# A fused attention and two-FFN kernel: three float64 weight blocks decoded in attention and not four, a first FFN that begins with two groups of two blocks, sums of values on GpSimd

## The chip, the core and the metric

One core of a Trainium2 chip runs the whole program. The metric is device time in microseconds (us) per execution; the times below are medians over runs. The core has five engines that work on their own queues and wait for each other through semaphores: TensorE (PE in the profile; its weight loads are PEld), VectorE (DVE), ScalarE (ACT), GpSimd (POOL) and SyncE (SP, which issues the DMAs).

## What is computed

```
mask   = q_bucket[:, :, :, None] == k_bucket[:, :, None, :]   # 6 sign bits of q@proj, k@proj
scores = where(mask, q @ k.T / 8, -1e9)                       # 2 batches, 8 heads, 768 x 768, d = 64
attn   = softmax(scores) @ v                                  # -> x: 1536 tokens x 512
h = x @ w_in; x = (h * tanh(softplus(h))) @ w_out             # first FFN, d_ff 2048, float64 weights
P = exp(x @ w_gate - max); 8 rounds of row and column normalising
out = sum over 8 experts e of  P[:, e] * (relu(x @ w1[e]) @ w2[e])   # d_ff 1024 each
```

[...] All large products run in fp32r, a reduced format of TensorE; an operand is split into a high part and the rest (`hi`, `lo`), and three products are added.

## The kernel before, in words

**Attention** (`attention()`, 32 units: 16 heads with two halves of 384 queries) is not written in the order in which it runs. Each piece of work is registered as a task with an engine (or two to choose from), a planned cost, a due time and the tasks that it follows; a greedy list scheduler at the end of the function takes the earliest one and emits it. So a task that changes its engine or cost shifts others too. Each unit has score tiles with row maxima (`s_mm`, `s_max`), transposed scores and their exponential (`st_mm`, `st_exp`), a split of the exponential (`split_hi`, `split_lo`), the product with the values (`av_count`, `av_mm`) and a normalisation (`norm`). A row whose bucket matches no key needs the plain sum over all values of its head: `vsum_red` adds up the six value chunks of two heads, `vsum_mm` adds over partitions, `vsum_fin` splits, `vsum_move` stores.

**Float64 decoding.** The first FFN has 16 blocks of 128 hidden columns; a block is 128 x 1024 words, loaded in two halves. `decode` turns a half into float32 in nine parts: sign (L135), absolute value (L137 on VectorE or L139 on ScalarE), low word (L141, ScalarE), clamp (L143), exponent (L147), sign back (L151), scale of the low word (L155), a product (L157, GpSimd) and a sum into `dec` (L159, VectorE). Then `convert_hi` (L171, ScalarE) writes the high part of a block into its place in a ring of 8 (`w0` to `w7`, of which `wx0` is number 2), and `convert_lo` (L176, GpSimd) the rest. In attention, `decode` tasks for the first `NATT` = 4 blocks are among those that the scheduler places, half n due at 10 + 11n; blocks 0 to 2 are also converted there, block 3 right after attention.

**First FFN** (the loop over `n` at the end of the listing). It is written in steps. A step is one weight block with one of three token blocks (`tb`, 512 tokens): `up(n)`, 12 matmuls into PSUM (L787 to L789: high weight with `xh`, high weight with `xl`, low weight with `xh`), `act(n)` (Mish and a cast on ScalarE L799, L800, the rest on VectorE L801), and `down` of step n - 3, 12 matmuls (L823) that add to four PSUM banks `y0` to `y3`. Blocks form `GROUPS` of four: a group goes over the three token blocks, and after its last block of a token block the four banks are added into `acc` by `evacuate` (the first group copies on ScalarE, L831; others add on VectorE, L833). In such a step `down` and `evacuate` stand ahead of `act`.

The remaining blocks are decoded in the steps: a list `early` gives each half a step d; parts 0 to 4 are written after `up(d)`, parts 5 to 7 at the end of step d, the last one at the end of step d + 1. A block is converted at the end of step d + 2 of its second half, behind whatever parts stand in that step. In the table below "decoded" gives the steps d of the two halves.

After it come a gate with its normalisation, expert 0 of both halves in the same loop (steps 48 to 71), and experts 1 to 7 in a Strassen form (L1122, L1185).

Of the kernel before, what the change touches and what calls it, by code (L numbers as in the profile page):

```python
# [7 lines left out]
F32 = mybir.dt.float32  # L8
# [5 lines left out]
ALU = mybir.AluOpType  # L14
AX = mybir.AxisListType

P = 128
B, H, S, D = 2, 8, 768, 64
# [10 lines left out]
NTB = NTOK // TB  # L29
BIG = float(2 ** 33)  # L30
N64 = 16
# [10 lines left out]
DUE0 = 10  # L42
PACE = 11
NX = 1
NATT = 4
FG = 4
LOW64 = float(2.0 ** -15)
HIGH64 = float(122880.0)
# [1 line left out]
RING_A = 2  # L50
# [7 lines left out]
def lsh_attention_moe_kernel(  # L58
# [13 lines left out]
    nc = tc.nc  # L72
# [23 lines left out]
    NW = N64 + NF  # L96
# [72 lines left out]
    def convert_hi():  # L169
        i = converted[0]  # L170
        nc.scalar.copy(ring[i % RING][:, 0, :], source(i))  # L171

    def convert_lo():
        i = converted[0]
        dst = ring[i % RING]
        nc.gpsimd.tensor_sub(dst[:, 1, :], source(i), f32(dst[:, 0, :]))  # L176
        converted[0] += 1
        if i >= N64:
            staged.pop(i)
            load_next()  # L180


    def attention():
        with ExitStack() as a:
# [4 lines left out]
            vs_p = a.enter_context(tc.tile_pool(name="vsp", bufs=1))  # L189
# [33 lines left out]
            vs_t = [None] * 4  # L223
# [126 lines left out]


            def vsum_red(h):
                vs_t[0] = vs_p.tile([P, 2, D], F32, tag="vs", name="vs")
                nc.vector.tensor_reduce(  # L354
                    out=vs_t[0], in_=vt[h // 2 % 2][:, :, 0:3:2, :].rearrange("p c a d -> p a d c"), axis=AX.X, op=ALU.add
                )

            def vsum_mm(h):
                vs_t[1] = ps_m.tile([P, 512], F32, tag="m", name="pvs")
# [165 lines left out]
            def task(engine, cost, due, f, *args, after=(), lag=None, ring=None, frees=None):  # L525
                tasks[f.__name__, *args] = (engine, cost, due, f, args, list(after), lag, ring, frees)
# [28 lines left out]
            for h in range(NH):  # L555
# [31 lines left out]
                task("Q", 0.6, vdue - 10, load_v, h, after=freed + [nm(clear, "vt", h // 2 % 2)] + [nm(prep_move, 0, j) for j in range(2, 6)] * (h < 2) + [nm(prep_move, 1, j) for j in range(6)] * (1 < h < 4), lag=1.3)  # L587
                if h % 2:
                    first = h >= 3
                    task("D", 0.9, vdue, vsum_red, h, after=[nm(load_v, h - 1), nm(load_v, h)] + [nm(vsum_mm, h - 2)] * first)  # L590
                    task("E", 0.11, vdue + 1, vsum_mm, h, after=[nm(vsum_red, h), nm(clear_start)], ring="m", frees=nm(vsum_fin, h))
                    task("D", 0.4, vdue + 2, vsum_fin, h, after=[nm(vsum_mm, h)] + [nm(vsum_move, h - 2, j) for j in range(2) if first])
                    for j in range(2):
                        task("Q", 0.6, vdue + 2.5, vsum_move, h, j, lag=0.01,
                             after=[nm(vsum_fin, h), nm(clear_start), nm(count_rows, 0), nm(count_rows, 1)]
                             + ([nm(av_count, 2 * prev + 1)] if prev >= 0 else []))
# [172 lines left out]
    hps, hid, yps = {}, {}, {}  # L769
    NST = NTB * NW  # L770

    GROUPS = [list(range(i, i + FG)) for i in range(0, NW, FG)]
    steps = [(g, tb, i) for g, c in enumerate(GROUPS) for tb in range(NTB) for i in c]
    NG = N64 // FG

    def step(n):
        g, tb, i = steps[n]
# [139 lines left out]

    LAG = 3
    blk = NTB * NF
    start_e = NG * NTB * FG  # L920
    for tb in range(NTB):
        n0 = start_e - (NTB - 1 - tb) * FG + LAG + 2
        at(n0, put(f"l{tb}", lambda tb=tb: logits(tb)))
# [118 lines left out]
    nxt = 0  # L1042
    nd = 0.0
    free_dec = {}
    convert_hi()
    convert_lo()
    for i in range(RING_A + NX + 1, NW):
        need = free[i - RING] + 1 if i >= RING else 0
        if NATT <= i < N64:
            nd = max(nd, free_dec.get(i - NDEC, 0))  # L1050
            for j in range(2):
                d = int(nd)
                for part, lag in enumerate((0, 0, 0, 0, 0, 0.5, 0.5, 0.5, 1.4)):
                    early.setdefault(d + lag, []).append((i, j, part, "D"))
                nd += 1.5
            need = max(need, d + 2)
        nxt = max(nxt, need)
        t = nxt
        at(t, convert_hi)
        at(t, convert_lo)  # L1060
        free_dec[i] = nxt + 1
        nxt += 1
# [247 lines left out]
```

## Time and profile before

| what | value |
|---|---|
| time, median of 3 runs | 1593.63 us (1593.13 to 1595.21) |
| the profiled execution | 1594.76 us; its span 1593.0 us |
| busy shares of the span | PE 98%, PEld 84%, DVE 54%, ACT 40%, POOL 54% |
| chain that ended last | PE 88%, DVE 8%, DMA 2%, issue 1%, ACT 1% |
| attention, then first FFN | 0 to 301.2 us, then steps of 24 matmuls |

The profile is one execution. "Busy" counts time with an instruction under way; for PE the ends of matmuls are modelled, so that overlapping matmuls fill its row. The chain is followed back from the last instruction, at each step to what released it. The difference between the execution's time and its span, 1.76 us, lies before the first and after the last instruction.

### The profile page before, as it was taken

The numbers are of one execution on the slowest core, as the hardware profiler recorded it, in microseconds if no ns is written. First come the engines' busy times: TensorE is split into PE (matmuls) and PEld (weight loads), VectorE is DVE, ScalarE is ACT, GpSimd is POOL, SyncE is SP. The second block draws the span as 40 slices with busy tenths as digits, with TensorE's granted clock in tenths as the row PEclk, the third lists the DMA queues.
The fourth block names the chain that finished last, engine by engine and source line by source line (L and its number), as shares of the span: only waits on it lengthen the run. The fifth ranks groups of instructions, "written<-read, shape, count | busy, mean of one in ns | idle before, by whom it ended". The sixth has DMA issues, their size and how long they took to land.

```text
span 1593.0 us, 20013 instructions
## 1 busy us (share of the span) xinstructions
PE 1557.7 (98%) x7407; PEld 1343.9 (84%) x7407; DVE 859.8 (54%) x1479; ACT 641.4 (40%) x1171; POOL 867.9 (54%) x694
## 2 busy tenths in 40 slices
PE   7889999999999999999999999999999999999999
PEld 5667787888888878889999989998998999998997
DVE  7999988687884222674433334455534243334243
ACT  4676777654333322223333333333333333333331
POOL 4778766432424340126565656666666666665652
PEclk7999999999999999999999999999999999999999
DMA  6754542022122010002222222222231222222221
GB/s 145 166 134 131 133 110 69 14 73 73 60 73 66 14 53 1 14 27 67 67 67 67 66 67 67 67 66 68 79 102 63 75 66 67 67 67 66 67 66 40
DMA packets 62641, 113.44 MB, mean 71 GB/s; under 512 B 18176, under 2 KB 18920, under 8 KB 62544
## 3 DMA queue, kind: packets, MB, share of 16 engines
q1 hardware_dynamic: 62544, 112.17, 24.1%
q8 instruction: 58, 0.95, 0.2%
q14 instruction: 39, 0.32, 0.1%
HBM read 89.22 MB, written 3.15 MB: 58 GB/s over the span
## 4 chain that ended last, share of the span: by engine, by line
PE 88%; DVE 8%; DMA 2%; issue 1%; ACT 1%; SPq 0%; POOL 0%; DVEq 0%; ACTq 0%
PE y L1185 29%; PE u L1122 26%; PE y L823 12%; PE h L787 4%; PE h L788 4%; PE h L789 4%; PE pav L487 3%; DVE mx L399 2%; PE ps L385 1%; PE pst L437 1%; DMA raw<-in_qk_dram 1%; PE pst L438 1%; DVE xu L516 1%; DVE col L404 0%; DVE vs L354 0%
## 5 line engine op out<-in xcount | busy, mean ns | idle before, releaser
L1185 PE MATMUL y<-w,gh 128*128 128x512 f32 x672 | 218.5, 393 | 0.0
L1185 PE MATMUL y<-ww,gh 128*128 128x512 f32 x672 | 218.1, 393 | 0.0
L1130 ACT ACTIVATE gh<-c 128x384 fp32r<-128x384 f32 x168 | 88.0, 526 | 278.1 <-DVE c L1142 278.1
L449 POOL TENSOR_TENSOR plo<-p,ph 128x384 fp32r<-128x384 f32 x128 | 140.0, 1104 | 71.9 <-ACT ph L446 42.7
L1185 PEld LDWEIGHTS y<-ww,gh 128*128 128x128 f32 x672 | 124.9, 188 | 18.1
L1185 PEld LDWEIGHTS y<-w,gh 128*128 128x128 f32 x672 | 124.8, 188 | 17.8
L1011 POOL TENSOR_TENSOR w<-stage,w 128x1024 fp32r<-128x1024 f32 x28 | 67.1, 2398 | 132.4 <-ACT w L1007 132.4
L1011 POOL TENSOR_TENSOR ww<-stage,ww 128x1024 fp32r<-128x1024 f32 x28 | 67.2, 2399 | 126.8 <-ACT ww L1007 126.8
L1185 PE MATMUL y<-w,gl 128*128 128x512 f32 x336 | 132.3, 394 | 0.0
L1185 PE MATMUL y<-ww,gl 128*128 128x512 f32 x336 | 132.2, 393 | 0.0
L1004 POOL TENSOR_TENSOR w<-sraw,w 128x1024 fp32r<-128x1024 f32 x28 | 67.4, 2406 | 107.4 <-ACT w L1000 107.4
L157 POOL TENSOR_TENSOR stage<-stage,sgn 128x512 f32<-128x512 f32 x32 | 46.0, 1437 | 123.3 <-DVE sgn L155 51.4
L1142 DVE TENSOR_TENSOR u<-u,p 128x384 f32<-128x384 f32 x56 | 31.2, 557 | 146.6 <-PE u L1122 146.6
L823 PE MATMUL y<-gh,w 128*128 128x512 f32 x336 | 110.2, 389 | 0.0
L443 ACT ACTIVATE p<-pst 128x384 f32<-128x384 f32 x192 | 91.9, 488 | 44.2 <-PE pst L438 39.4
L787 PE MATMUL h<-xh,w 128*128 128x512 f32 x252 | 99.5, 395 | 0.0
L399 DVE TENSOR_REDUCE mx<-ps 128x1 f32<-128x768 f32 x95 | 89.8, 946 | 17.5 <-PE ps L385 16.9
L788 PE MATMUL h<-xl,w 128*128 128x512 f32 x252 | 98.2, 390 | 0.0
L789 PE MATMUL h<-xh,w 128*128 128x512 f32 x252 | 98.2, 390 | 0.0
L1135 DVE SCALAR_TENSOR_TENSOR gl<-c,gh 128x384 fp32r<-128x384 f32 x168 | 94.2, 561 | 6.0 <-ACT gh L1130 0.2
L1130 ACT ACTIVATE gh<-u 128x384 fp32r<-128x384 f32 x56 | 27.6, 492 | 161.9 <-PE u L1122 161.9
L1135 DVE SCALAR_TENSOR_TENSOR gl<-u,gh 128x384 fp32r<-128x384 f32 x56 | 31.2, 557 | 109.8 <-ACT gh L1130 109.7
(245 smaller groups left out, 4054.5 us busy)
## 6 DMA issues: line engine op xcount, KB each, us to landing
stage<-in_w_dram SPq DMA_DIRECT2D x152, 512.0 KB
raw<-in_qk_dram SPq DMA_DIRECT2D x13, 384.0 KB
wx<-hi SPq DMA_DIRECT2D x20, 192.0 KB
vt<-in_v_dram SPq DMA_DIRECT2D x16, 192.0 KB
out_dram<-acc SPq DMA_DIRECT2D x12, 256.0 KB
zq<-hi SPq DMA_DIRECT2D x11, 192.0 KB
ak<-hi SPq DMA_DIRECT2D x11, 192.0 KB
zq<-lo SPq DMA_DIRECT2D x11, 192.0 KB
```

The costliest lines, as they stand in the source:

```text
L399: nc.vector.tensor_reduce(out=m[:, t:t + 1], in_=s_t[t][:, :, :HALF], axis=AX.XY, op=ALU.max)
L443: nc.scalar.activation(p_t[u, c], st_t.pop((u, c))[:, :HALF], AF.Exp, scale=0.125)
L449: (nc.gpsimd if e == "P" else nc.vector).tensor_sub(out, in0, in1)
L787: nc.tensor.matmul(t, wt[:, 0, f], xh[:, kc, c], start=(kc == 0), stop=False)
L788: nc.tensor.matmul(t, wt[:, 0, f], xl[:, kc, c], start=False, stop=False)
L789: nc.tensor.matmul(t, wt[:, 1, f], xh[:, kc, c], start=False, stop=(kc == KC - 1))
L823: nc.tensor.matmul(yps[j], x, y, start=(head and m == 0), stop=(tail and m == 2))
L1011: nc.gpsimd.tensor_sub(y[:, 1, :], t, f32(y)[:, 0, :])
L1122: nc.tensor.matmul(bank[x], weight(u, a, m, kc), moving(u, b, mm, kc), start=(first and n == 0), stop=(n == 5), skip_group_check=not first)
L1130: nc.scalar.activation(hi, src, AF.Relu)
L1135: nc.vector.scalar_tensor_tensor(out=lo, in0=src, scalar=0.0, in1=f32(hid_u[u, c][0]), op0=ALU.max, op1=ALU.subtract)
L1185: nc.tensor.matmul(y_t[t], (hi, hi, lo)[m][:, t % 3 * P:(t % 3 + 1) * P], y, start=(k == 0 and first and m == 0), stop=(k == NF // 2 - 1 a ...
```

## The change

`NATT` goes from 4 to 3: the scheduler in attention places `decode` tasks for three blocks, and block 3 is decoded and converted in the first steps of the FFN, where halves of blocks under 8 are now 1.4 steps apart. `GROUPS` begins with two groups of two blocks. `vsum_red` becomes three GpSimd additions (of 384, 128 and 128 elements on a partition). Between `vsum_red` and the planning of the conversions, lines of the changed kernel are numbered two higher.

```diff
-NATT = 4
+NATT = 3
...
             def vsum_red(h):
-                vs_t[0] = vs_p.tile([P, 2, D], F32, tag="vs", name="vs")
-                nc.vector.tensor_reduce(
-                    out=vs_t[0], in_=vt[h // 2 % 2][:, :, 0:3:2, :].rearrange("p c a d -> p a d c"), axis=AX.X, op=ALU.add
-                )
+                s = vs_p.tile([P, 3, 2, D], F32, tag="vs", name="vs")
+                v = vt[h // 2 % 2][:, :, 0:3:2, :]
+                nc.gpsimd.tensor_add(s, v[:, 0:3], v[:, 3:6])
+                nc.gpsimd.tensor_add(s[:, 0], s[:, 0], s[:, 1])
+                nc.gpsimd.tensor_add(s[:, 0], s[:, 0], s[:, 2])
+                vs_t[0] = s[:, 0]
...
-                    task("D", 0.9, vdue, vsum_red, h, ...)
+                    task("P", 1.9, vdue, vsum_red, h, ...)
...
-    GROUPS = [list(range(i, i + FG)) for i in range(0, NW, FG)]
+    GROUPS = [[0, 1], [2, 3]] + [list(range(i, i + FG)) for i in range(4, NW, FG)]
-    NG = N64 // FG
+    NG = 1 + N64 // FG
-    start_e = NG * NTB * FG
+    start_e = N64 * NTB
...
-    convert_hi()
-    convert_lo()
-    for i in range(RING_A + NX + 1, NW):
+    for i in range(RING_A + NX, NW):
         need = free[i - RING] + 1 if i >= RING else 0
         if NATT <= i < N64:
             nd = max(nd, free_dec.get(i - NDEC, 0))
             for j in range(2):
                 d = int(nd)
                 for part, lag in enumerate((0, 0, 0, 0, 0, 0.5, 0.5, 0.5, 1.4)):
                     early.setdefault(d + lag, []).append((i, j, part, "D"))
-                nd += 1.5
+                nd += 1.4 if i < 8 else 1.5
             need = max(need, d + 2)
```

What this loop and `GROUPS` give for the blocks of which the text speaks (step numbers, counted from the code):

| block | decoded, before | converted after step | first used in step | decoded, now | converted after step | first used in step |
|---|---|---|---|---|---|---|
| 3 | in attention | ahead of step 0 | 3 | 0, 1 | 3 | 7 |
| 4 | 0, 1 | 3 | 12 | 2, 4 | 6 | 12 |
| 7 | 9, 10 | 12 | 15 | 11, 12 | 14 | 15 |
| 9 | 15, 16 | 18 | 25 | 17, 18 | 20 | 25 |
| 11 | 21, 22 | 24 | 27 | 23, 24 | 26 | 27 |
| 13 | 27, 28 | 30 | 37 | 29, 30 | 32 | 37 |
| 15 | 33, 34 | 36 | 39 | 35, 36 | 38 | 39 |

`evacuate` follows the last block of a token block three steps later: before after steps 6, 10, 14 (copies) and 18, 22, 26, ..., 38; now after 4, 6, 8 (copies), 10, 12, 14 (VectorE) and then 18, 22, 26, ..., 38.

The ScalarE queue of the FFN around block 7: `L171` is its high part, `L799` (now `L801`) the Mish of a step, which reads that step's `h`. Before, with the Mish of steps 13, 14 and 15 behind it:

```order
L171 CAST w7_3780<-dec3_85 128x1024
L141 ACTIVATE stage_4195<-stage_4195 128x512
L799 ACTIVATE t_4299<-h_4279 128x512
L800 CAST gh_4297<-t_4299 128x512
L831 COPY acc_3781<-y0_4219 128x512
L831 COPY acc_3781<-y1_4223 128x512
L831 COPY acc_3781<-y2_4227 128x512
L831 COPY acc_3781<-y3_4231 128x512
L799 ACTIVATE t_4352<-h_4321 128x512
L800 CAST gh_4350<-t_4352 128x512
L141 ACTIVATE stage_4236<-stage_4236 128x512
L799 ACTIVATE t_4379<-h_4359 128x512
```

Now, with the Mish of steps 14 and 15:

```order
L801 ACTIVATE t_4376<-h_4340 128x512
L802 CAST gh_4374<-t_4376 128x512
L171 CAST w7_3774<-dec3_85 128x1024
L141 ACTIVATE stage_4297<-stage_4297 128x512
L801 ACTIVATE t_4405<-h_4385 128x512
```

The conversion stood behind the Mish of step 12 and now stands behind that of step 14, right ahead of the step that uses `w7`.

In the GpSimd queue the low part `L176` of block 7 stands, as before, behind the product `L157` of the first half of block 8 (`stage_4209`; `stage_4166` is the second half of block 7). Now:

```order
L176 TENSOR_TENSOR w6_3773<-dec2_84,w6_3773 128x1024
L157 TENSOR_TENSOR stage_4166<-stage_4166,sgn1_87 128x512
L157 TENSOR_TENSOR stage_4209<-stage_4209,sgn0_86 128x512
L176 TENSOR_TENSOR w7_3774<-dec3_85,w7_3774 128x1024
L157 TENSOR_TENSOR stage_4297<-stage_4297,sgn1_87 128x512
```

That product needs `L155` of the same half, which in the VectorE queue of step 14 now stands behind the four additions of `evacuate` (`L835`) and behind the rest of `act(14)` (`gl_4375`):

```order
L147 TENSOR_SCALAR stage_4209<-stage_4209 128x512
L835 TENSOR_TENSOR acc_3775<-y0_4321,acc_3775 128x512
L835 TENSOR_TENSOR acc_3775<-y1_4325,acc_3775 128x512
L835 TENSOR_TENSOR acc_3775<-y2_4329,acc_3775 128x512
L835 TENSOR_TENSOR acc_3775<-y3_4333,acc_3775 128x512
L803 TENSOR_TENSOR gl_4375<-t_4376,gh_4374 128x512
L151 SCALAR_TENSOR_TENSOR stage_4209<-stage_4209,sgn0_86 128x512
L155 TENSOR_SCALAR sgn0_86<-stage_4209 128x512
```

Before, the two parts of a half in step 12 (`stage_4111`) had no additions ahead of them, since the first group's banks were copied by ScalarE:

```order
L143 TENSOR_SCALAR stage_4111<-stage_4111 128x512
L147 TENSOR_SCALAR stage_4111<-stage_4111 128x512
L801 TENSOR_TENSOR gl_4257<-t_4258,gh_4256 128x512
L151 SCALAR_TENSOR_TENSOR stage_4111<-stage_4111,sgn0_86 128x512
L155 TENSOR_SCALAR sgn0_86<-stage_4111 128x512
```

And TensorE's queue at `up(15)` now, with the waits that stand in it: the first matmul waits for the high part, the third for the low one.

```order
L825 MATMUL y3_4333<-gl_4230,w3_3770 128x512
L825 MATMUL y3_4333<-gh_4229,w3_3770 128x512
L789 MATMUL h_4385<-xh_74,w7_3774 128x512 [waits Activation_49]
L790 MATMUL h_4385<-xl_75,w7_3774 128x512
L791 MATMUL h_4385<-xh_74,w7_3774 128x512 [waits Pool_49]
```

The same queue has these two waits at `up(7)`, `up(27)` and `up(39)`, for blocks 3, 11 and 15. Over attention as a whole the scheduler also moves some tasks with two possible engines: `split_v`'s low part goes from 3 on VectorE and 13 on GpSimd to 11 and 5, and casts `ph` on VectorE go from 35 to 39.

## Rows read from the trace of the kernel before

**Rows 1.** Windows: stretch, length, busy us (instructions) of each engine, PEclk, DMA, GB/s.

```profile
120.00:160.00 40.00, 36.42 (x173) 28.98 (x173) 39.14 (x65) 27.34 (x62) 32.28 (x28) 0.99 0.48 127
...
200.00:240.00 40.00, 38.45 (x192) 32.33 (x191) 32.99 (x64) 28.42 (x64) 26.16 (x24) 1.00 0.42 111
```

**Rows 2.** Timeline, PE: `av_count` (L472) of units 2, 12, 16, 29; the FFN's first matmul.

```profile
46.53 0.44 PE L472 MATMUL pav<-wx,vf 4*128 4x384 f32 x1
...
141.86 0.44 PE L472 MATMUL pav<-sq,vf 4*128 4x384 f32 x1
...
178.90 0.43 PE L472 MATMUL pav<-sq,vf 4*128 4x384 f32 x1
...
283.52 0.44 PE L472 MATMUL pav<-sq,vf 4*128 4x384 f32 x1
...
301.22 0.69 PE L787 MATMUL h<-xh,w 128*128 128x512 f32 x1
```

**Rows 3.** Chain that ended last, 85 to 260 us: start, us, what.

```profile
127.95 1.44 DVE vs L354
...
218.24 1.50 DVE vs L354
```

**Rows 4.** Windows of the tile `stage` alone, the stretch of block 3's two halves: DVE, ACT, POOL.

```profile
149.00:178.10 29.10, 11.21 (x14) 0.00 (x0) 2.60 (x2) 1.00 0.50 131
```

**Rows 5.** Groups by line and form, 0 to 302 us: busy us, mean ns, idle before.

```profile
L449 POOL TENSOR_TENSOR plo<-p,ph 128x384 fp32r<-128x384 f32 x128 | 140.0, 1104 | 71.9 <-ACT ph L446 42.7 <-DVE ph L446 24.7 <-DVE nr L506 4.4
...
L446 DVE CAST ph<-p 128x384 fp32r<-128x384 f32 x35 | 17.2, 494 | 5.1 <-ACT p L443 2.7 <-PE pav L487 1.6 <-PE ps L385 0.2
...
L354 DVE TENSOR_REDUCE vs<-vt 128x128 f32<-128x768 f32 x8 | 12.0, 1503 | 0.0
L449 POOL TENSOR_TENSOR vl<-vt,vh 128x256 fp32r<-128x256 f32 x13 | 11.5, 889 | 9.7 <-ACT vh L446 9.7
...
L449 DVE TENSOR_TENSOR vl<-vt,vh 128x256 fp32r<-128x256 f32 x3 | 1.3, 425 | 0.1
```

**Rows 6.** Line L516 in attention: instructions, ns shortest/median/longest, first and last start.

```profile
L516 DVE TENSOR_TENSOR xu<-xu,rs x15: 530/548/2192, 71.5 to 300.3; 128x384 f32<-128x384 f32 x15
```

**Rows 7.** Timeline, steps 18 to 20: `down` evacuated, block 9 converted, `up(19)`, `up(20)`.

```profile
394.92 2.73 DVE L833 TENSOR_TENSOR acc<-y,acc 128x512 f32<-128x512 f32 x4 [1.82 <-PE y L823]
...
396.76 0.39 PE L787 MATMUL h<-xh,w 128*128 128x512 f32 x1
...
397.21 0.39 PE L789 MATMUL h<-xh,w 128*128 128x512 f32 x1
...
398.16 0.69 DVE L151 SCALAR_TENSOR_TENSOR stage<-stage,sgn 128x512 int32<-128x512 int32 x1
...
399.45 1.38 POOL L157 TENSOR_TENSOR stage<-stage,sgn 128x512 f32<-128x512 f32 x1 [9.27 <-issue]
...
400.79 2.57 POOL L176 TENSOR_TENSOR w<-dec,w 128x1024 fp32r<-128x1024 f32 x1
...
402.20 0.39 PE L787 MATMUL h<-xh,w 128*128 128x512 f32 x1
```

**Rows 8.** Timeline, POOL, low parts of block 13 (after step 30) and 17 (after step 38).

```profile
466.06 2.57 POOL L176 TENSOR_TENSOR w<-dec,w 128x1024 fp32r<-128x1024 f32 x1
...
505.31 2.41 POOL L176 TENSOR_TENSOR w<-stage,w 128x1024 fp32r<-128x1024 f32 x1 [3.04 <-ACT w L171]
```

**Rows 9.** Windows of the FFN, steps 9 to 14.

```profile
342.40:375.00 32.60, 32.60 (x146) 27.00 (x144) 23.30 (x35) 13.64 (x22) 12.41 (x7) 1.00 0.26 81
```

**Rows 10.** Timeline, PE around a wait in attention, and windows after it.

```profile
114.44 0.69 PE L385 MATMUL ps<-bk,sq 96*128 96x384 f32 x1 [2.21 <-DVE mx L399]
...
114.50:120.50 6.00, 6.00 (x19) 6.00 (x20) 4.39 (x12) 3.52 (x7) 3.03 (x3) 0.50 0.40 99
121.00:127.00 6.00, 6.00 (x31) 4.92 (x30) 5.44 (x9) 5.34 (x13) 5.73 (x5) 1.00 0.52 139
```

More of the change, by code (lines that the diff above doesn't have):

```diff
@@ L589, in attention @@
                     first = h >= 3
-                    task("D", 0.9, vdue, vsum_red, h, after=[nm(load_v, h - 1), nm(load_v, h)] + [nm(vsum_mm, h - 2)] * first)
+                    task("P", 1.9, vdue, vsum_red, h, after=[nm(load_v, h - 1), nm(load_v, h)] + [nm(vsum_mm, h - 2)] * first)
                     task("E", 0.11, vdue + 1, vsum_mm, h, after=[nm(vsum_red, h), nm(clear_start)], ring="m", frees=nm(vsum_fin, h))
```

## The prediction

> **What bounds the kernel.** I read the windows by stage first, then the chain, then the timeline of the FFN. In attention there are two stages. While weights are decoded VectorE is busy for 39.1 of 40 us and TensorE for 36.4; once that is over TensorE has 38.5 and VectorE 33.0 [rows 1]. The starts of `av_count` give the pace [rows 2]: units 2 to 12 take 95.3 us (9.53 each), units 12 to 16, which hold the decoding of block 3, 37.0 us (9.26 each), units 16 to 29 104.6 us (8.05 each). The chain goes through the value sums in both stages [rows 3]. The FFN begins at 301.22 [rows 2] and is TensorE alone: a step is 402.20 - 396.76 = 5.44 us [rows 7], its PE row has no gap (32.60 of 32.60 in steps 9 to 14, [rows 9]), and the later expert stages lean on TensorE as well (PE is 98% busy over the span). So time taken from attention comes off the end, and any wait of TensorE in the FFN is added to it in full.
>
> **Attention, what is removed.** Block 3's two halves cost VectorE 11.2 us in 14 instructions and GpSimd 2.6 us in 2 [rows 4]. The eight value sums cost VectorE 8 x 1.503 = 12.0 us [rows 5].
>
> **Attention, what is added.** GpSimd gets eight times one addition of 384 elements and two of 128. The first is priced as `plo`, 1.10 us [rows 5]; of 128 elements there is no row, so a third of that (0.37) and the 0.89 of a 256-element `vl` bound it; I take 0.4, since GpSimd's time grows about with its elements in these rows. That is 1.9 us a sum, 15.2 in all (14.7 to 23.0). The scheduler gives part of VectorE's time back: eight `vl` at 0.425 (3.4 us) and four `ph` casts at 0.494 (2.0). The remaining exchanges are single tasks in both directions, left at nothing. VectorE thus loses 23.2 - 5.4 = 17.8 us net, and GpSimd gains 15.2 - 2.6 - 8 x 0.889 = 5.5 us, which its idle time can hold (32.3 busy of 40 at most, [rows 1]).
>
> **Attention, what that is worth.** Without block 3, units 12 to 16 have no decoding and should run at the later pace: 4 x (9.26 - 8.05) = 4.8 us. The value sums stand on the chain at about 1.45 us each; two lie in the stretch before (2.9 us), two in the TensorE stage, where TensorE is 96% busy and a second chain runs close behind, so I count half of 3.0. Sum 9.2, taken as 9. Upper bound: all of VectorE's net 17.8. Lower bound 4, worked out under the port below. The scheduler shuffles everything else too, which no row prices; the bounds have to carry that.
>
> **The FFN, early steps.** Three things are late next if something is. Token block 1 is now read at step 2, 5.4 us after the start, and block 2 at step 4, but attention finishes its halves in that order, and nothing in the code puts work between. Block 3 is converted after step 3 and used in step 7, about four steps later. Block 4 to 6 keep three or more steps. The twelve further evacuations fall to VectorE after steps 10, 12, 14; each set of four takes 2.73 us [rows 7] while the next `up` covers 2.72 us, as after step 18 now. I price all this at nothing; were the cover gone, one set would show up to 2.7 us.
>
> **The FFN, blocks 7, 11 and 15.** This is the part that decides. Each of them is now converted at the end of the step ahead of its first use, where there were three steps between. How late a low part is after such a step stands in the trace: block 9 is converted after step 18, one in which banks are evacuated by VectorE and the next block's first half is under way, just like blocks 7 and 11 now. There [rows 7] the four additions last until 397.65, `L151` starts at 398.16, the product `L157` at 399.45, and the low part runs from 400.79 to 403.36. The third matmul of the next `up`, which would have needed it, started at 397.21. So that wait is 403.36 - 397.21 = 6.15 us. Block 13, after step 30, gives the same: it ends at 466.06 + 2.57 = 468.63 [rows 8], and that step's third matmul is at 397.21 + 12 x 5.44 = 462.49, 6.14 us earlier. I take 6.2 us for steps 15 and 27 each, with the release.
>
> At step 15 VectorE may be later still: it was busy 23.3 of 32.6 us in steps 9 to 14 [rows 9], and gets 12 x 0.68 = 8.2 us of additions and a slightly denser decoding, which fills it. I add 0.7 (0 to 2). At step 39 no half of another block is in GpSimd's queue; the trace has that case after step 38, where the low part ends at 505.31 + 2.41 = 507.72 [rows 8] against 397.21 + 20 x 5.44 = 506.01: 1.7 us. What is queued behind the waiting matmul is all of TensorE's work; the other engines catch up in the wait, so it happens once per block. Sum: 6.2 + 0.7 + 6.2 + 1.7 = 14.8 us (14.1 to 16.1).
>
> **The clock after a wait.** In attention TensorE waited 2.21 us for VectorE, and its granted clock then stood at 0.50 (1.2 GHz) for the six microseconds from 114.5 to 120.5 although it worked all the time, and at 1.00 (2.4 GHz) from 121.0 [rows 10]. Waits of 6 us are longer than that one, so I expect the same after steps 15 and 27: six microseconds at half speed do the work of three, 3.0 us each. The wait at step 39 is shorter than 2.21 us; I leave it at nothing (0 to 3.0). Sum 6.0 (0 to 9.0).
>
> **Sum.** -9 + 14.8 + 6.0 = +11.8 us. On the profiled execution, 1594.76, that is 1606.6; this execution is 1.13 us over the median of the runs, so against the median 1593.63 it is 1605.4 us, 0.74% slower. What a measurement can tell from no change is about 0.2%, 3.2 us.
>
> **Rivals.**
>
> *The clock stays up.* The drop at 114 is a single case. Then only 14.8 - 9 = +5.8: 1599.4 us. Against it: the waits here are three times as long.
>
> *GpSimd blocks VectorE.* VectorE instructions that last 0.55 us at the median reach 2.19 [rows 6]. If every microsecond that GpSimd is busy more (5.5) held up VectorE, the gain in attention falls from 9 to about 4: 14.8 + 6.0 - 4 = +16.8, 1610.4 us. The Trainium skill, page SBUF — State Buffer, section Who interferes with whom, has such a rule: VectorE and GpSimd share a pair of ports that one instruction holds to its end; VectorE instructions with two SBUF inputs are blocked by it, a `tensor_reduce` never. By that rule the change swaps a sum that cannot collide for three that can. The spread of [rows 6] agrees with it; how much of GpSimd's time hits such an instruction no row tells.
>
> *Only the conversion itself is waited for.* This ends on the other side. If the products of the next half were through GpSimd before the high part is written, blocks 7 and 11 would wait as block 15 does: 3 x 1.7 = 5.1 us, too short to pull the clock down by the one case there is, and 5.1 - 9 = -3.9: 1589.7 us, faster. It decides when VectorE does `L151` and `L155` ahead of the four additions, that is before the last matmul of `down`. Against it stands the written order: both are behind the additions, and the additions wait for that matmul.
>
> *Attention gains more.* If all of VectorE's 17.8 us came off, the result would be +3.0: 1596.6 us. Against it: TensorE's pace of 8.05 us a unit is a floor that block 3's stretch reaches after 4.8.
>
> **Chances.** The forecast 0.58; the clock stays up 0.13; GpSimd blocks 0.11; attention gains much more 0.06; only the conversion 0.05; further waits in the FFN, around evacuation and decoding, beyond 1612 us 0.07. The range from 1597 to 1614 us leaves out the third rival, most of the last case and the tail of the fourth. The likeliest case's own range, with attention between 5 and 13 and a third clock drop or not, is 1601 to 1612. Faster by over 0.2%: the third rival and a little of the fourth, 0.06. Within 0.2%: the rest of the fourth and a clock that stays up with a good attention, 0.10. Slower 0.84.
>
> **What would show it.** The first FFN matmul near 292 us and not 301.2; units in the stretch of the former block 3 at about 8 us. Three waits of `L791` for GpSimd's `L176`, of about 7, 6 and 2 us, at steps 15, 27 and 39, and none at step 7; a PEclk of 0.5 for some 6 us after the first two. Everything between at 5.44 us a step. I would be wrong in the main step if these waits are absent or under 2 us, in the second if PEclk stays 1.0 behind them, and in the first if the FFN starts later than 298 or before 286 us.

## The result, and the profile after

The changed kernel takes 1608.65 us (median of 4 runs, 1608.48 to 1609.32) against 1593.8 us for the kernel before on the same chip: ratio 1.0092, interval 1.0079 to 1.0104, slower. Its profiled execution takes 1608.48 us with a span of 1606.7 us, 13.7 us more than the span of before.

The page of the changed kernel: busy shares, and the group of the matmuls with the low part (busy us, mean ns, idle before).

```profile
PE 1558.7 (97%) x7407; PEld 1342.1 (84%) x7407; DVE 866.3 (54%) x1497; ACT 638.4 (40%) x1165; POOL 877.2 (55%) x710
...
L791 PE MATMUL h<-xh,w 128*128 128x512 f32 x252 | 100.1, 397 | 13.7 <-POOL w L176 13.7
```

The engine shares hardly differ from before; the answer is in the last row. TensorE sat idle ahead of `L791` for 13.7 us; before, no matmul of the FFN waited for a low part. To place the rest, I read the same starts as [rows 2], from the timeline of PE after: `av_count` of units 2, 12, 16 and 29, and the FFN's first matmul.

```profile
43.66 0.44 PE L474 MATMUL pav<-wx,vf 4*128 4x384 f32 x1
...
141.24 0.43 PE L474 MATMUL pav<-sq,vf 4*128 4x384 f32 x1
...
172.97 0.43 PE L474 MATMUL pav<-sq,vf 4*128 4x384 f32 x1
...
278.85 0.44 PE L474 MATMUL pav<-sq,vf 4*128 4x384 f32 x1
...
296.55 0.69 PE L789 MATMUL h<-xh,w 128*128 128x512 f32 x1
...
370.32 0.39 PE L789 MATMUL h<-xh,w 128*128 128x512 f32 x1
...
377.09 0.80 PE L791 MATMUL h<-xh,w 128*128 128x512 f32 x1 [6.15 <-POOL w L176]
...
383.56 0.39 PE L789 MATMUL h<-xh,w 128*128 128x512 f32 x1
...
443.40 0.39 PE L789 MATMUL h<-xh,w 128*128 128x512 f32 x1
...
449.96 0.79 PE L791 MATMUL h<-xh,w 128*128 128x512 f32 x1 [5.95 <-POOL w L176]
...
457.48 0.39 PE L789 MATMUL h<-xh,w 128*128 128x512 f32 x1
...
517.32 0.39 PE L789 MATMUL h<-xh,w 128*128 128x512 f32 x1
...
519.50 0.50 PE L791 MATMUL h<-xh,w 128*128 128x512 f32 x1 [1.56 <-POOL w L176]
...
524.66 0.39 PE L789 MATMUL h<-xh,w 128*128 128x512 f32 x1
```

**Attention ends 4.67 us earlier** (296.55 against 301.22, one execution each), in pieces of both signs:

| stretch | before, us | after, us | difference |
|---|---|---|---|
| start to unit 2 | 46.53 | 43.66 | -2.87 |
| units 2 to 12 | 95.33 | 97.58 | +2.25 |
| units 12 to 16 (block 3 before) | 37.04 | 31.73 | -5.31 |
| units 16 to 29 | 104.62 | 105.88 | +1.26 |
| unit 29 to the FFN | 17.70 | 17.70 | 0 |

**The FFN gives back 18.4 us in three steps.** Step 15 lasts 383.56 - 370.32 = 13.24 us where an undisturbed step takes 5.44, so 7.80 more; step 27 14.08 (8.64 more); step 39 7.34 (1.90 more). In each, the third matmul should start 0.45 us after the first [rows 7]. It starts 6.32, 6.11 and 1.73 us later than that, 14.16 in all. The remaining 4.18 us come behind the waits. From the first expert matmul of the later stages to the end both kernels take 887.3 us, so nothing else differs: -4.67 + 14.16 + 4.18 = +13.7. The profiled execution of before is 1.0 us slower than its median, so against the medians (14.85 us) the gain in attention is rather 3.5 to 3.7; the groups-alone kernel below shows that second number.

Windows of the changed kernel, columns as in [rows 1]: the two stretches shown there, and those behind the first, the second and the third wait.

```profile
120.00:160.00 40.00, 37.36 (x183) 30.41 (x181) 36.73 (x63) 29.23 (x66) 33.49 (x32) 1.00 0.52 140
200.00:240.00 40.00, 38.46 (x192) 32.43 (x192) 33.89 (x62) 29.67 (x66) 27.52 (x26) 1.00 0.47 119
...
377.00:380.00 3.00, 2.91 (x7) 2.33 (x8) 0.75 (x2) 0.00 (x0) 0.04 (x1) 0.50 0.03 5
380.00:385.00 5.00, 5.00 (x24) 4.12 (x23) 2.32 (x4) 1.22 (x2) 0.19 (x1) 1.00 0.06 7
450.00:455.00 5.00, 5.00 (x12) 3.93 (x13) 0.63 (x2) 0.37 (x1) 0.00 (x0) 0.50 0.00 0
456.00:457.00 1.00, 1.00 (x6) 0.82 (x5) 1.00 (x2) 0.00 (x0) 0.00 (x0) 1.00 0.00 0
...
520.00:521.00 1.00, 1.00 (x6) 0.78 (x5) 0.00 (x0) 0.00 (x0) 0.00 (x0) 1.00 0.00 0
```

In attention GpSimd has a little more to do than in [rows 1] (33.49 and 27.52 us, 32.28 and 26.16 before), and VectorE less only in the first stretch. After the first wait TensorE works for 3 us at 0.50 (1.2 GHz), after the second for 5 us, after the third at 1.00 at once. Half of 3 and of 5 is 4.0 us, which is the 4.18 but for 0.2.

How the first wait arises, from the timeline of the changed kernel, all engines, at step 14's end:

```profile
366.61 0.69 DVE L159 TENSOR_TENSOR dec<-stage 128x512 f32<-128x512 f32 x1 [1.20 <-POOL stage L157]
...
368.94 2.48 DVE L835 TENSOR_TENSOR acc<-y,acc 128x512 f32<-128x512 f32 x4
368.96 1.05 ACT L171 CAST w<-dec 128x1024 fp32r<-128x1024 f32 x1
...
371.93 0.69 DVE L151 SCALAR_TENSOR_TENSOR stage<-stage,sgn 128x512 int32<-128x512 int32 x1
372.65 0.43 DVE L155 TENSOR_SCALAR sgn<-stage 128x512 int32<-128x512 int32 x1
373.21 1.34 POOL L157 TENSOR_TENSOR stage<-stage,sgn 128x512 f32<-128x512 f32 x1 [6.64 <-issue]
374.52 2.52 POOL L176 TENSOR_TENSOR w<-dec,w 128x1024 fp32r<-128x1024 f32 x1
```

Block 7's `dec` is complete at 367.30 and its high part is written by 370.01. GpSimd is idle by then, but next in its queue is `L157` of block 8. That needs `L155`, which on VectorE stands behind the four additions and `L151`. So the low part starts at 374.52, although both its inputs were ready 4.5 us earlier. Had it started then, it would have ended near 372.5 and not at 377.04.

### The profile page after: what moved, and what is told of

Read it like the earlier page. It is cut to its first block, busy times and chain, and to the rows that moved or that the text cites. A ratio compares the mean times of both kernels' runs of the same rounds, so it can differ in the third digit from the quotient of the medians.

```text
span 1606.7 us, 20036 instructions
## 1 busy us (share of the span) xinstructions
PE 1558.7 (97%) x7407; PEld 1342.1 (84%) x7407; DVE 866.3 (54%) x1497; ACT 638.4 (40%) x1165; POOL 877.2 (55%) x710
## 4 chain that ended last, share of the span: by engine, by line
PE 69%; DVE 1%; issue 1%; POOL 0%; ACT 0%; POOLq 0%; DVEq 0%
PE y L1185 29%; PE u L1122 26%; PE y L825 7%; PE h L791 2%; PE h L789 2%; PE h L790 2%; PE lg L851 0%; PE lt L862 0%; POOL w L176 0%; DVE stage L143 0%; DVE stage L137 0%; DVE prob L901 0%; DVE gl L806 0%; DVE prob L900 0%; POOL stage L157 0%
## 5 line engine op out<-in xcount | busy, mean ns | idle before, releaser
L1185 PEld LDWEIGHTS y<-w,gh 128*128 128x128 f32 x672 | 124.8, 188 | 17.8
L157 POOL TENSOR_TENSOR stage<-stage,sgn 128x512 f32<-128x512 f32 x32 | 44.3, 1384 | 150.2 <-DVE sgn L155 61.5
L791 PE MATMUL h<-xh,w 128*128 128x512 f32 x252 | 100.1, 397 | 13.7 <-POOL w L176 13.7
L401 DVE TENSOR_REDUCE mx<-ps 128x1 f32<-128x768 f32 x95 | 90.0, 947 | 19.6 <-PE ps L387 19.2
```

The costliest lines, as they stand in the source:

```text
L401: nc.vector.tensor_reduce(out=m[:, t:t + 1], in_=s_t[t][:, :, :HALF], axis=AX.XY, op=ALU.max)
L791: nc.tensor.matmul(t, wt[:, 1, f], xh[:, kc, c], start=False, stop=(kc == KC - 1))
L1185: nc.tensor.matmul(y_t[t], (hi, hi, lo)[m][:, t % 3 * P:(t % 3 + 1) * P], y, start=(k == 0 and first and m == 0), stop=(k == NF // 2 - 1 a ...
```

## The experiments

### The FFN: where the 18 us come from

**The conversion ahead of the next half's parts.** The only edit moves the parts that end a step behind the conversions in that step:

```diff
-        for t in early.pop(n + 0.4, []) + early.pop(n + 0.5, []):
-            decode(*t)
...
+        for t in early.pop(n + 0.4, []) + early.pop(n + 0.5, []):
+            decode(*t)
```

> The changed kernel with one thing moved: at the end of a step the conversion is written ahead of the parts of the half in progress, so that the low part of blocks 7 and 11 is not behind the next half's product in GpSimd's queue. Theory (the queue order makes 4.5 of the 6.2 us): all three waits are 1.6 to 2.2 us, too short for the clock to fall, and the time is 1608.6 - 2 x 4.4 - 4.0 = 1596 us. Rival (the conversion itself is that late): waits of 6 us stay, time about 1608. If the clock falls behind waits of 2 us as well, some 1600.

Measured 1595.93 us, ratio 1.001 [1.0001, 1.002], with attention as in the changed kernel (FFN from 296.68). Timeline of this kernel at the same place, and the first of its three waits:

```profile
369.09 1.05 ACT L171 CAST w<-dec 128x1024 fp32r<-128x1024 f32 x1
369.84 2.48 DVE L835 TENSOR_TENSOR acc<-y,acc 128x512 f32<-128x512 f32 x4
370.21 2.37 POOL L176 TENSOR_TENSOR w<-dec,w 128x1024 fp32r<-128x1024 f32 x1 [2.75 <-ACT w L171]
372.64 0.50 PE L791 MATMUL h<-xh,w 128*128 128x512 f32 x1 [1.57 <-POOL w L176]
...
439.78 0.50 PE L791 MATMUL h<-xh,w 128*128 128x512 f32 x1 [1.56 <-POOL w L176]
...
506.93 0.50 PE L791 MATMUL h<-xh,w 128*128 128x512 f32 x1 [1.56 <-POOL w L176]
```

The low part now follows the high part at once, and the three waits are alike, some 1.56 us each. PEclk is 1.00 behind all of them. So 12.7 of the 14.9 us of slowdown hung on one place in a queue and on the clock behind it, with no work saved; the FFN alone shortens from 422.82 to 410.06 us. This is the rival "only the conversion itself is waited for", made by hand.

**The conversion a step earlier.** The rule that sets the step of the conversion allows one step less:

```diff
-            need = max(need, d + 2)
+            need = max(need, d + 1)
```

> The changed kernel with every block converted one step earlier, at the end of the step in which its last decode part stands (after step 13 and not 14 for block 7). If the late conversion is all that the FFN lost, TensorE waits for no low part, the clock stays at 1.0, the FFN takes the 404.4 us of the kernel before up to the Strassen stage, and the time is 1608.6 - 18.4 = 1590.2, less than before by 0.2%. Rival, from the run with denser decoding: ScalarE now waits in its queue for VectorE's last part ahead of the Mish, and TensorE waits for that; then 1593 us or more.

Measured 1591.46 us, ratio 0.9985 [0.9976, 0.9994]: the fastest version that leaves no work out, 17.2 us below the changed kernel and 0.15% below the one before. FFN from 296.85, and its length is 405.52 us against 404.45 before. Of the waits of TensorE in the FFN, which were all to go, this kernel has one; 0.3 us of the 1.07 us that its FFN is longer than before stay unexplained:

```profile
PE h L791 <- POOL w L176: 0.7, 1, 0.7
```

**The groups alone**, in the kernel before, with block 3 still decoded in attention:

```diff
-    GROUPS = [list(range(i, i + FG)) for i in range(0, NW, FG)]
+    GROUPS = [[0, 1], [2, 3]] + [list(range(i, i + FG)) for i in range(4, NW, FG)]
```

> The kernel before with the two groups of two blocks alone: four blocks decoded in attention, sums on VectorE, conversions where they were (after step 12 for block 7). The prediction priced twelve more evacuations on VectorE at nothing, and counted the loss to the conversions alone: FFN of 404.4 us to the Strassen stage, no wait of TensorE, the same time as before. Rival (the denser evacuation is part of the loss): waits for y banks or low parts in steps 5 to 16, FFN 406 us or more.

Measured 1593.87 us, ratio 0.9994 [0.9984, 1.0003]; the FFN takes 404.44 us, as before, without a wait of TensorE. The twelve further evacuations on VectorE are hidden, as the prediction priced them. This kernel's attention is that of before, yet its profiled execution starts the FFN at 300.22 us and not at 301.22. The clock differs: TensorE has the same wait in both, 2.21 us [rows 10] and 2.22 us, but behind it the half clock ends between 117.5 and 118.0 us here and between 120.5 and 121.0 in the execution of before. So differences of 1 us between two FFN starts are not told from chance.

**Decoding a little denser**: the halves of blocks 3 to 7 are 1.2 steps apart.

```diff
-                nd += 1.4 if i < 8 else 1.5
+                nd += 1.2 if i < 8 else 1.5
```

> The changed kernel with halves of blocks under 8 spaced 1.2 steps and not 1.4, so that blocks 7, 11 and 15 are converted after steps 12, 24 and 36 as in the kernel before. If the late conversions and the clock behind them are the whole loss in the FFN (about 14.2 and 4.0 us), no third matmul waits for GpSimd, PEclk stays 1.0 and the time is 1590.4 +- 1.5 us. Rival, VectorE is the limit with twelve more additions and a denser decoding: other waits of TensorE for VectorE or GpSimd appear in steps 5 to 16, and the time is 1593 us or more.

Measured 1595.08 us, ratio 1.0009 [0.9999, 1.0018]. All three waits of `L791` are gone, but the FFN still takes 409.71 us, for another one has come: the time is the rival's, its cause is not. Timeline of this kernel, ScalarE and PE:

```profile
354.14 0.67 ACT L141 ACTIVATE stage<-stage 128x512 f32<-128x512 uint32 x1 [2.71 <-DMA stage<-in_w_dram]
354.85 0.47 PE L825 MATMUL y<-gh,wx 128*128 128x512 f32 x1 [3.38 <-ACT stage L141]
```

ScalarE waited 2.71 us for a weight half that was still being loaded. The `gh` that `down` needs is also ScalarE's work, and TensorE lost 3.38 us and then its full clock (0.50 from 356 to 358 us). So this earlier decoding ran into its load; no run loads the half earlier as well.

### Attention: why 4.7 us and not 9

**The sums alone**, in the kernel before (the diff of `vsum_red` and its `task` line alone).

```diff
-                    task("D", 0.9, vdue, vsum_red, h, ...)
+                    task("P", 1.9, vdue, vsum_red, h, ...)
```

> The kernel before with the value sums on GpSimd and nothing else of the change. The prediction's sum (a sum on VectorE's chain is worth 1.45 us, half of that in the TensorE stage) would have the FFN begin 4.4 us earlier, at 296.8 us, and the time at 1589.4. Theory A, formed from the two traces: the sums gained nothing, since units 2 to 12 and 16 to 29 did not get shorter; FFN at 301 +- 1.5 us, time 1593 +- 1.5. Theory B, GpSimd's sums hold up VectorE: FFN at 303 us or later, time 1596 or more.

Measured 1594.4 us, ratio 1.0009 [0.9999, 1.0018]. The FFN starts at 300.37, 0.85 us earlier, and takes 404.47 us. That is what theory A expected; beside the 300.22 of the groups-alone kernel the sums gained nothing that can be told from chance.

**All but the sums**: the changed kernel, with `vsum_red` and its task as before (the same diff, read backwards).

> The changed kernel with the value sums back on VectorE, as before. Prediction's sum: the FFN begins 4.4 us later than in the changed kernel, at 301 us, time 1613. Theory A (the sums are worth nothing, block 3 is the whole gain): FFN at 296.5 +- 1.5 us, time 1608.5 +- 1.5. Theory B (the sums on GpSimd cost something): FFN at 292 to 294 us, time 1604 to 1606. The three waits for low parts stay at 6.2, 6.0 and 1.6 us in all of them.

Measured 1611.52 us, ratio 1.0113 [1.0098, 1.0128]. The FFN starts at 299.9, only 1.3 us earlier than before; units 12 to 16 took 33.55 us, 3.5 less than before, but units 16 to 29 1.3 more. The FFN has the same three waits, 13.7 us. So the sums have no part in the waits of the FFN; it is 424.26 us long, 1.4 more than in the changed kernel, with longer half clocks behind the same waits. The start is nearest to the prediction's sum (301); theories A and B are out. Against the start of before, taking block 3 out is worth 1.3 us alone, moving the sums 0.85 us alone, and both together 4.7; against 300.22 it is 0.3, nothing and 3.7. Either way the parts do not add up. That this comes from the scheduler, which lays out everything anew each time, is likely but not shown.

**A shorter sum on VectorE**, in the kernel before: two of the six chunks are added.

```diff
-                    out=vs_t[0], in_=vt[h // 2 % 2][:, :, 0:3:2, :].rearrange("p c a d -> p a d c"), axis=AX.X, op=ALU.add
+                    out=vs_t[0], in_=vt[h // 2 % 2][:, 0:2, 0:3:2, :].rearrange("p c a d -> p a d c"), axis=AX.X, op=ALU.add
```

> The kernel before, in its own order, with the value sum over two of the six chunks only (the sum is left incomplete): about 0.5 us and not 1.5 on VectorE, nothing else touched. The prediction priced a sum by its place on the chain: by that this is worth some two thirds of its 4.4 us, so the FFN begins at 298 us. Rival: a second chain (TensorE, ScalarE and GpSimd of other units) runs so close behind that it is worth under 1 us, FFN at 300.3 us or later.

Measured 1590.79 us, ratio 0.9981 [0.9972, 0.999]; the FFN starts at 298.01, 3.2 us earlier. A sum on VectorE does cost what the chain [rows 3] made of it.

**A shorter sum on GpSimd**, in the changed kernel: one addition of 128 elements in place of three additions, all planned times kept.

```diff
-                nc.gpsimd.tensor_add(s, v[:, 0:3], v[:, 3:6])
-                nc.gpsimd.tensor_add(s[:, 0], s[:, 0], s[:, 1])
-                nc.gpsimd.tensor_add(s[:, 0], s[:, 0], s[:, 2])
+                nc.gpsimd.tensor_add(s[:, 0], v[:, 0], v[:, 3])
```

> The changed kernel, in its own order, with one GpSimd addition of 128 elements and not three additions (the sum is left incomplete): some 0.4 us and not 1.9 on GpSimd, eight times. If GpSimd's time or its holding up VectorE ate the gain in attention, the FFN begins 3 us or more earlier than 296.6, at 293.5 or before. If not, within 1 us of 296.6.

Measured 1604.42 us, ratio 1.0065 [1.005, 1.0081]. The timeline of PE of this kernel, the places of the first list:

```profile
42.74 0.43 PE L472 MATMUL pav<-wx,vf 4*128 4x384 f32 x1
...
137.72 0.44 PE L472 MATMUL pav<-sq,vf 4*128 4x384 f32 x1
...
169.42 0.44 PE L472 MATMUL pav<-sq,vf 4*128 4x384 f32 x1
...
273.71 0.44 PE L472 MATMUL pav<-sq,vf 4*128 4x384 f32 x1
...
291.42 0.69 PE L787 MATMUL h<-xh,w 128*128 128x512 f32 x1
```

The FFN starts 5.13 us earlier than in the changed kernel, 9.80 earlier than before. The gain lies where the changed kernel had lost: units 2 to 12 take 94.98 us (97.58 in the changed kernel), units 16 to 29 104.29 (105.88), and the stretch to unit 2 0.92 less. Units 12 to 16 take 31.70, as in the changed kernel. So GpSimd's additions cost 5 us, and without them the forecast of 9 would have been met.

**The order of before, with GpSimd additions**: in the kernel before, `vsum_red` has its three GpSimd additions, but the task is still planned as VectorE's, so nothing moves.

```diff
...
-                nc.vector.tensor_reduce(
-                    out=vs_t[0], in_=vt[h // 2 % 2][:, :, 0:3:2, :].rearrange("p c a d -> p a d c"), axis=AX.X, op=ALU.add
-                )
+                nc.gpsimd.tensor_add(s, v[:, 0:3], v[:, 3:6])
...
                     task("D", 0.9, vdue, vsum_red, h, ...)
```

> The kernel before, in its own planned order, with the sums done by GpSimd at the places that were planned for VectorE. The run with the sums planned on GpSimd began the FFN at 300.4 us. If it is the scheduler's shuffling that ate the gain, the FFN begins at 297 to 298 us here. If GpSimd's time (its additions stand ahead of plo in the queue) eats it, at 301 us or later.

Measured 1597.63 us, ratio 1.0023 [1.0014, 1.0032]; the FFN starts at 303.71, 2.5 us later than before. With no shuffling at all, taking 12.0 us of work off VectorE [rows 5] and putting it on GpSimd is a loss, and the short sum above brings the gain back in the new order. So it is not the new order that ate the gain. Windows of all of attention, the kernel before and then this one, columns as in [rows 1]:

```profile
0.00:301.22 301.22, 270.72 (x1245) 217.76 (x1245) 258.98 (x445) 204.26 (x446) 205.78 (x189) 0.95 0.48 117
...
0.00:303.71 303.71, 272.81 (x1244) 218.41 (x1245) 254.16 (x437) 203.77 (x446) 222.10 (x213) 0.99 0.47 116
```

VectorE does the same instructions but for the eight sums, so 258.98 - 12.0 = 247.0 us were left to do, and they took 254.16: 7.2 of the 12.0 us come back as longer instructions. Not all of that need be GpSimd's additions: in the version with the short sum on VectorE, where GpSimd has nothing more to do, the same instructions take some 250 us (253.34, of which the sums are 3.3).

**GpSimd's queue or its reads?** In the changed kernel one addition of 128 elements and four memsets, which take GpSimd about as long as the three additions (16.2 us in attention against 17.9); the memsets read nothing.

```diff
-                nc.gpsimd.tensor_add(s, v[:, 0:3], v[:, 3:6])
-                nc.gpsimd.tensor_add(s[:, 0], s[:, 0], s[:, 1])
-                nc.gpsimd.tensor_add(s[:, 0], s[:, 0], s[:, 2])
+                nc.gpsimd.tensor_add(s[:, 0], v[:, 0], v[:, 3])
+                for _ in range(4):
+                    nc.gpsimd.memset(s[:, 1:3], 0.0)
```

> The changed kernel in its own order, with one GpSimd addition of 128 elements and four memsets of 256 elements (0.32 us each) in place of the three additions, so that GpSimd is busy about as long as with the whole sum and reads almost nothing (the sum is left incomplete). With the short sum alone the FFN began at 291.4 us, with the whole sum at 296.6. If the time in GpSimd's queue is what costs, it begins at 295.5 to 297 us; if it is VectorE held up by GpSimd's additions, at 291.5 to 293 us; between them, both.

Measured 1607.53 us, ratio 1.0085 [1.0072, 1.0098]; the FFN starts at 294.72, between 291.42 (short sum) and 296.55 (full sum). So 3.3 of the 5.1 us are there without the reads. Windows of all of attention in the changed kernel, with the memsets and with the short sum:

```profile
0.00:296.55 296.55, 267.04 (x1245) 213.64 (x1245) 251.10 (x437) 200.30 (x438) 213.82 (x203) 0.97 0.47 116
...
0.00:294.72 294.72, 267.77 (x1245) 214.15 (x1245) 249.16 (x437) 200.47 (x438) 211.51 (x219) 0.99 0.47 116
...
0.00:291.42 291.42, 267.61 (x1244) 214.00 (x1245) 246.77 (x437) 200.61 (x438) 201.93 (x187) 0.99 0.48 118
```

VectorE has the same 437 instructions in all three, and the memsets too make them longer: 2.4 us more than with the short sum, against 4.3 us with the full one. So this run does not part the time in GpSimd's queue from the delay of VectorE. Both stay possible as the larger part.

### Other places for the sum

**On TensorE**: six accumulating matmuls with a column of ones in place of one, no `vsum_red` (and the earlier conversion of above).

```diff
-                nc.tensor.matmul(vs_t[1][0:1, 0:P], ones[:, 0:1], vs_t[0].rearrange("p a d -> p (a d)"), start=True, stop=True)
+                v = vt[h // 2 % 2][:, :, 0:3:2, :]
+                for c in range(NKC):
+                    nc.tensor.matmul(
+                        vs_t[1][0:1, 0:P].rearrange("p (a d) -> p a d", a=2), ones[:, 0:1], v[:, c], start=(c == 0), stop=(c == NKC - 1)
+                    )
```

> Three blocks decoded, blocks converted one step earlier, and the value sum taken off VectorE and GpSimd both: six small matmuls with a column of ones add the six chunks in PSUM. By the run with a short sum on GpSimd, attention without a sum in either queue ends at 291 us; the matmuls cost TensorE about five times 0.2 us eight times, of which the three in its own stage should show in full. FFN at 292 to 295 us, time 1587 to 1590, faster than both kernels. Rival: TensorE's extra 8 us show in full, FFN at 297 us or later, 1592 or more.

Measured 1595.66 us, ratio 1.001 [1.0002, 1.0019]; the FFN starts at 300.42. By groups, 0 to 300 us of this kernel:

```profile
L356 PE MATMUL pvs<-vt,ones 128*1 128x128 f32 x96 | 13.0, 290 | 0.0
```

These are the rival's numbers (297 us or later, 1592 or more). In the changed kernel these are 16 matmuls with 3.0 us; the 10.0 us more are busy time on the engine that has least to spare. How much of the 3.6 us that the start lies later than in the version above is theirs, and how much the new order's, no run tells.

**As three additions on VectorE** (and the earlier conversion).

```diff
-                nc.gpsimd.tensor_add(s, v[:, 0:3], v[:, 3:6])
+                nc.vector.tensor_add(s, v[:, 0:3], v[:, 3:6])
...
-                    task("P", 1.9, vdue, vsum_red, h, ...)
+                    task("D", 0.9, vdue, vsum_red, h, ...)
```

> Three blocks decoded, blocks converted one step earlier, and the three additions done by VectorE in place of the one reduction of 1.5 us. By rows of VectorE's additions (0.56 us for 384 elements, about 0.28 for 128) the sum is 1.1 us, 0.4 less, eight times. With the reduction on VectorE the FFN began at 299.9 us; the short sum gave 3.2 us for 8 x 1.0. Expected: FFN at 298.5 us, time 1592. Rival: the additions wait for GpSimd at the shared port and last as long as the reduction, FFN at 300 us or later, 1594 or more.

Measured 1603.29 us (1600.15 to 1607.65), ratio 1.0059 [1.0044, 1.0074]. The profiled execution is the longest of these; its FFN starts at 313.08. Durations of the two short additions in it, shortest, median and longest in ns:

```profile
L356 DVE TENSOR_TENSOR vs<-vs x8: 293/982/1281, 18.5 to 261.5; 128x128 f32<-128x128 f32 x8
...
L357 DVE TENSOR_TENSOR vs<-vs x8: 292/840/1781, 19.2 to 262.6; 128x128 f32<-128x128 f32 x8
```

An addition that can be done in 0.29 us takes 0.98 at the median, and the first, of 384 elements, 0.54, so the three cost 2.36 us where the one reduction took 1.50 [rows 5]. Eight times the difference is 6.9 us; the start is 13.2 us later than with the reduction (299.9), and the rest is not traced. PEclk in attention falls to 0.87 from 80 to 120 us and 0.94 from 160 to 200; the longer waits of TensorE come with a lower clock.

## Why the prediction was right, and what in it was wrong

**The FFN, blocks 7, 11 and 15: right.** Forecast 6.2 + 0.7, 6.2 and 1.7 us; measured 6.32, 6.11 and 1.73. Reading the lateness of a low part off a block that was converted the same way but not yet needed (blocks 9, 13, 17; [rows 7, 8]) gave each wait to 0.1 us, except for the 0.7 added at step 15. That extra was wrong: VectorE did the additions in 2.48 us, no slower than the 2.73 of [rows 7]. The order of conversion and parts as cause is shown by the run that swaps them and by the one that converts earlier. No wait at step 7, as forecast.

**The early steps and the groups: right,** at nothing (the run with the groups alone).

**The clock after a wait: right in kind, mis-sized.** Forecast six microseconds at 0.50 after each of two waits, 6.0 us; the rows show 3 and 5, worth 4.0. The single case of [rows 10] was too little to size it; the same wait in the groups-alone kernel was followed by about 3.5 us. That the wait of 1.56 us leaves the clock alone was right. The rival "the clock stays up" is out.

**Attention: right in sign, half the size.** The step that failed is "GpSimd gains 5.5 us, which its idle time can hold". Block 3 itself was priced well in its own stretch (5.3 against 4.8), though alone it brings 1.3 or less at the end of attention. The sums were to bring 4.4 and cost 0.64 instead (-2.87 + 2.25 + 1.26, with the first stretch counted to them). The run with the short GpSimd sum puts the difference, 5.1 us, on GpSimd's additions; the short VectorE sum shows that the gain side had been priced right. The rival "GpSimd blocks VectorE" has the size (a gain of 4; measured 4.7, or 3.7 from 300.22), and the measured time, 1608.65 us, is nearer to its 1610.4 than to the forecast's 1605.4. That VectorE is held up is shown below at two places; how much of the 5.1 us comes that way and how much through GpSimd's queue stays open. VectorE's net relief was too large as well: 17.8 us forecast, 258.98 - 251.10 = 7.9 measured.

GpSimd's time was also underpriced. Its groups in attention, changed kernel:

```profile
L355 POOL TENSOR_TENSOR vs<-vt 128x384 f32<-128x384 f32 x8 | 9.2, 1148 | 7.2 <-DMA vt<-in_v_dram 7.2
...
L357 POOL TENSOR_TENSOR vs<-vs 128x128 f32<-128x128 f32 x8 | 4.5, 558 | 0.6
L356 POOL TENSOR_TENSOR vs<-vs 128x128 f32<-128x128 f32 x8 | 4.2, 524 | 0.6
```

That is 2.2 us a sum where 1.9 was taken, 17.9 us in all, inside the bounds. The 0.4 for 128 elements came from reading GpSimd's time as growing with its elements; a line through the two rows that it used, 0.889 us for 256 and 1.104 for 384, gives 0.67, and 0.52 and 0.56 were measured. In all GpSimd is busy for 8.0 us more in attention, not 5.5. And a mean share of a window says little: GpSimd is busy for 213.8 of the 296.55 us, so over a quarter of its time is free, and yet its additions cost 5 us.

How the blocking looks, from the timeline of the changed kernel, DVE, POOL and PE:

```profile
182.20 0.94 DVE L401 TENSOR_REDUCE mx<-ps 128x1 f32<-128x768 f32 x1
182.35 1.01 POOL L451 TENSOR_TENSOR plo<-p,ph 128x384 fp32r<-128x384 f32 x1 [0.30 <-DVE ph L448]
...
183.32 1.31 POOL L355 TENSOR_TENSOR vs<-vt 128x384 f32<-128x384 f32 x1
...
183.70 0.95 DVE L406 TENSOR_SCALAR col<-mx 128x3 f32<-128x3 f32 x1
...
184.78 0.28 PE L422 MATMUL prow<-idt,col 128*12 128x128 f32 x1 [1.37 <-DVE col L409]
```

`L406` handles three elements on a partition and takes 0.17 us at the median. Here it takes 0.95 and ends at 184.65, 0.02 us after GpSimd's addition (183.32 + 1.31 = 184.63), and TensorE waits 1.37 us for what comes behind it. The same happens at 249.33. With the short sum it takes 0.41 us at this place, again to the end of GpSimd's addition, and TensorE waits 0.85 us. The row maxima `L401` keep their 0.94 us beside a GpSimd addition. The Trainium skill, page SBUF — State Buffer, section Who interferes with whom, says of this chip that a `tensor_scalar` can contend with GpSimd for a pair of ports that they share, that a `tensor_reduce` never does, and that a VectorE instruction with two inputs from SBUF does when the GpSimd instruction reads SBUF. The trace agrees with the first two, and with the third in the version with three additions on VectorE (0.29 to 1.28 us for the same one).

**The sum.** Forecast -9 + 14.8 + 6.0 = +11.8; measured -4.7 + 14.2 + 4.2 = +13.7 between the two profiled executions. An error of +4.3 in attention and one of -2.5 in the FFN offset each other in part; that the total is nearer than its terms is luck.

## What to carry to other kernels

When a producer moves nearer to its consumer, look for work of the same kind that is in its new place already: how late it ends there is the coming wait. Before paying for such a wait, check what stands ahead of the late instruction in its own queue; here a swap of two lines removed 13 us, and converting a step earlier made the change a gain. An idle share does not say that an engine can take more work: look at who is queued behind the new work, and on GpSimd also at which VectorE instructions run beside it. And before reading a difference of 1 us between two traces, look for two traces of the same code.

## What the runs showed of the hardware that was not expected

The time at half clock after a wait is not fixed, not even for the same wait: about 6.5 us after 2.21 us of waiting in the kernel before [rows 10] and about 3.5 after the same wait in the groups-alone kernel; in the FFN 3 us after 6.15 us in the changed kernel and some 5 after the same wait with all but the sums. The four waits of 1.56 us in the FFN of the kernel with the conversion ahead and of the changed one left the clock at full speed.

A VectorE instruction of three elements beside a GpSimd addition ends with it, at 0.95 us in place of 0.17 at the median, and at 0.41 beside a shorter addition.
